# Where two key buffers begin: 128 bytes of room in front of each, in an attention and FFN kernel

## The chip, the core and the metric

The kernel runs on one core of a Trainium2 chip. Its time is the device time of one execution in microseconds; the time given for a kernel is the median of several executions. Beside the times there is a trace of one execution, taken by the hardware profiler, and all rows shown come from it. TensorE (PE) multiplies, with weight loads (PEld) issued by the same sequencer; VectorE (DVE), ScalarE (ACT) and GpSimd (POOL) do the rest; SyncE (SP) issues the DMAs.

## The reference

Attention over pooled keys and values, and behind it a two-layer FFN with softplus, all in float32:

```python
# q, k, v: (8 batches, 8 heads, 576 rows, 64); w_in: (512, 2048); w_out: (2048, 512)
k_p = k.reshape(B, H, 72, 8, D).mean(axis=3)      # 576 rows pooled to 72
v_p = v.reshape(B, H, 72, 8, D).mean(axis=3)
scores = (1 / sqrt(D)) * q @ k_p.transpose(0, 1, 3, 2)
scores = scores - scores.max(axis=-1, keepdims=True)
attn = exp(scores); attn = attn / (attn.sum(axis=-1, keepdims=True) + 1e-9)
x = heads side by side of (attn @ v_p)            # (8 * 576, 512)
h = x @ w_in
g = maximum(h, 0) + log1p(exp(-abs(h)))
out = g @ w_out                                   # (4608, 512)
```

## The kernel before

The 4608 rows of x are worked off in 18 chunks of 256 rows (`CT`), each in two tiles of 128. The chunks 0 to 2 go one way through the FFN (lines 619 to 646), chunk 3 mostly like the later ones but with line 713 for its second layer, and from chunk 4 on the FFN is the steady one: in eight steps, each with 24 matmuls of the first layer (`pair1`, line 672) and 21 of the second (`pair2_fast`, line 821), all with a weight of 128 x 128 and 256 columns streamed. Every product is made of three matmuls, of high and low parts.

While TensorE does the FFN of chunk c, it also does the attention of chunk c + 1 in between: the transposes of q (line 384), the scores (`pair_scores`, line 512), the transposes of the probabilities (lines 465 and 565) and the attention-value products (`av_products`, lines 591 and 598). In the chunks 0 to 3 the scores are line 404. A chunk has one stage of scores, of 64 matmuls; each takes 64 rows of the array, 64 columns, and streams 72 columns of keys:

```python
b = (x.first + i * P // 2) // S                                    # line 511: the batch of these 64 rows
o = nc.tensor.matmul(out=ps[r, n * SP:(n + 1) * SP], lhsT=x.q[js, m, r],
                     rhs=kT[b % 2][js, m], ...)
```

So the rows of an even batch read the buffer kT0, those of an odd batch kT1. As a batch has 576 rows, 2.25 chunks, some chunks lie in one batch and some in two. In a stage, all of the first tile's matmuls but one come ahead of the second tile's (`order` in `pair_scores`; the one head's two matmuls of the second tile stand at the two ends). The keys of a batch are pooled by DVE, transposed by TensorE (line 256) and written to kT by ACT (`k_scaled`, line 262), once for each batch.

The order of all work on TensorE, ACT, DVE and SP is written out by a planner (`Order`), which knows of each operation its engine, an assumed cost, what it follows and which slots it needs; it doesn't know where in memory a tile lies.

Where a tile lies follows from the order in which it is asked for. A pool puts its tiles one after the other, and the pools stand one behind the other: `const`, `wpool`, `xpool`, `one`, `small`. Tiles that no instruction reads or writes keep their bytes; the kernel uses such tiles (`fill`, line 220) to shift what comes after. In the program as built, these tiles begin at these bytes of each partition:

| tile | bytes | begins at | modulo 256 |
|---|---|---|---|
| kT0 (keys, even batches) | 1152 | 2240 | 192 |
| kT1 (keys, odd batches) | 1152 | 3392 | 64 |
| vs0, vs1 (values) | 1024 each | 4544, 5568 | 192 |
| vlo0, vlo1 (the last values) | 2048 each | 6592, 8640 | 192 |
| fill of 64 floats | 256 | 10688 | 192 |
| w (weights) | 90240 | 10944 | 192 |
| l (weights, staging) | 41088 | 102080 | 192 |

The other tiles come behind these. The q that the scores load as weights lies in two buffers at multiples of 512.

Of the kernel before, what the change touches and what calls it, by code (L numbers as in the profile page):

```python
# [9 lines left out]
F32 = mybir.dt.float32  # L10
# [98 lines left out]
def pooled_attention_softplus_ffn(  # L109
# [14 lines left out]
    P = 128  # L124
    POOL = 8
    SP = S // POOL
# [4 lines left out]
    HP = H // 2  # L131
# [10 lines left out]
    const = ctx.enter_context(tc.tile_pool(name="const", bufs=1))  # L142
    wpool = ctx.enter_context(tc.tile_pool(name="wpool", bufs=1))
# [42 lines left out]
    band(zl[:, 0:4 * KL].rearrange("p (n y) -> p n y", n=4), POOL, KM)  # L186

    SCALE = -1.0 / (POOL * D ** 0.5)
    kT = [const.tile([P, HP, SP], F32, name=f"kT{i}") for i in range(2)]

    vs = [const.tile([P, HP, D], F32, name=f"vs{i}") for i in range(2)]
    vlo = [const.tile([3 * 4 * KL, HP, P], F32R, name=f"vlo{i}") for i in range(2)]
# [4 lines left out]

    PART, ROOM, LATE = 2 * DM, 16, 5
    BEGINS = [0, FC - LATE, FC]
    FILL = 256 - ROOM, 32, 16, 64  # L200
    groups = [None, None]

    def group(f):
        g = 0 if f < FC - LATE else 1
        n = BEGINS[g + 1] - BEGINS[g]
        if groups[g] is None:
            groups[g] = wpool.tile([P, 2 * (n * PART + ROOM)], F32R, tag="wl"[g], name="wl"[g])
        return groups[g], f - BEGINS[g], n
# [9 lines left out]
        return w[:, (n + f) * PART:(n + f + 1) * PART]  # L218

    fill = lambda pool, n, i: n and pool.tile([P, n], F32, tag=f"fill{i}", name="fill")  # L220
    fill(wpool, FILL[3], 3)
    group(0)
    fill(wpool, FILL[0] - ROOM, 0)
    stage = wpool.tile([P, 2 * (LATE * PART + ROOM)], I32, tag="l", name="stage")
    stage_at = lambda i: stage[:, i * 2 * PART:(i + 1) * 2 * PART].rearrange("p (i n) -> p i n", i=2)
    fill(wpool, FILL[1], 1)
    for tag in ("Xha", "Xhb", "Xla", "Xlb"):
        xpool.tile([P, HP, CT], F32R, tag=tag, name="x")
    fill(xpool, FILL[2], 2)
    wi, wo = {}, {}  # L230
# [1332 lines left out]
```

## Time and profile before

| | us |
|---|---|
| median of 3 runs | 888.52 |
| lowest and highest run | 888.02, 890.73 |
| the profiled execution | 889.17 |
| its span, from the first to the last instruction | 887.4 |
| TensorE busy in the span | 874.7 |

In the rows of the profile, "PE h L672" is TensorE's work of line 672 on a tile named h, and x24 says how many instructions stand together. In the chain of waits each row has the start in us from the span's beginning, the length in us, and what ran; the length of a row is the time by which the chain moved on, so that a row of 24 matmuls divided by 24 is the distance from one matmul to the next. The duration of a single matmul in the groups is longer than this distance, as matmuls overlap.

### The profile page before, as it was taken

To read this page: it belongs to the slowest core of one execution; us is meant where nothing else is said; L and a number is where in the kernel's file an instruction comes from. 1 tells how busy PE (TensorE), PEld (TensorE's weight loads), DVE (VectorE), ACT (ScalarE), POOL (GpSimd) and SP (SyncE) were. 2 spreads that over 40 slices of the span, in tenths; PEclk is the share of its full clock that TensorE was granted. 3 is DMA by queue.
4 is the path that set the end of the run, shared out by engine and by line. 5 is a ranking of instruction groups with operands and counts; after the bars stand their busy time and mean duration, and the time that the engine had idled before them with its cause. 6 is when DMAs were issued, how large, how long until landed. Compare 5 with 4: busy or idle time off the path is not lost.

```text
span 887.4 us, 20500 instructions
## 1 busy us (share of the span) xinstructions
PE 874.7 (99%) x8280; PEld 831.5 (94%) x8280; DVE 645.2 (73%) x1601; ACT 417.9 (47%) x852; POOL 3.8 (0%) x33
## 2 busy tenths in 40 slices
PE   7999999999999999999999999999999999999997
PEld 3789989899899999999999999999999999999997
DVE  5899999888866868687767766778566564747454
ACT  5964433445454544544444445353545344444432
POOL 1000000000000000000000000000000000000000
PEclk9999999999999999999999999999999999999999
DMA  8975544545889678578757675677566556646472
GB/s 237 312 236 192 189 149 164 172 159 192 273 281 228 237 227 278 195 258 250 243 190 248 240 232 197 224 244 251 196 205 223 180 205 202 223 153 229 168 249 83
DMA packets 107086, 191.12 MB, mean 215 GB/s; under 512 B 46064, under 2 KB 60400, under 8 KB 106992
## 3 DMA queue, kind: packets, MB, share of 16 engines
q1 hardware_dynamic: 106992, 189.82, 63.6%
q8 instruction: 65, 1.06, 0.5%
q14 instruction: 29, 0.24, 0.1%
HBM read 167.25 MB, written 22.54 MB: 214 GB/s over the span
## 4 chain that ended last, share of the span: by engine, by line
PE 96%; DVE 1%; DMA 1%; ACT 1%; issue 0%; SPq 0%; DVEq 0%; ACTq 0%
PE h L672 38%; PE m L821 30%; PE acc L646 7%; PE h L624 7%; PE acc L713 3%; PE avp L591 2%; PE qTp L384 2%; PE ptp L465 2%; PE sc L512 1%; PE avp L598 1%; PE kps L1056 1%; DMA kvl<-in_v_dram 1%; DMA kvst<-in_k_dram 1%; ACT E L429 0%; PE m L512 0%; PE ltp L565 0%
## 5 line engine op out<-in xcount | busy, mean ns | idle before, releaser
L672 PE MATMUL h<-x,l 128*128 128x256 f32 x2748 | 337.9, 279 | 0.0
L672 PEld LDWEIGHTS h<-x,l 128*128 128x128 f32 x2748 | 323.9, 188 | 1.1
L680 ACT ACTIVATE g<-h 128x512 f32<-128x512 f32 x120 | 71.9, 599 | 267.4 <-PE h L672 267.2
L821 PE MATMUL m<-w,so 128*128 128x256 f32 x1134 | 148.3, 278 | 0.0
L821 PEld LDWEIGHTS m<-w,so 128*128 128x128 f32 x1134 | 138.3, 188 | 0.1
L731 DVE TENSOR_TENSOR sf<-g 128x128 f32<-128x128 f32 x112 | 32.7, 292 | 138.2 <-ACT g L680 138.2
L745 ACT CAST so<-sf 128x512 fp32r<-128x512 f32 x112 | 69.8, 623 | 69.2 <-DVE sf L734 68.4
L821 PE MATMUL m<-w,gh 128*128 128x256 f32 x476 | 91.9, 281 | 0.0
L750 DVE TENSOR_TENSOR so<-sf,so 128x512 fp32r<-128x512 f32 x112 | 77.3, 690 | 18.3 <-ACT so L745 16.6
L821 PEld LDWEIGHTS m<-w,gh 128*128 128x128 f32 x476 | 72.0, 188 | 0.0
L701 DVE TENSOR_TENSOR gl<-g,gh 128x384 fp32r<-128x384 f32 (+1 forms) x120 | 67.3, 561 | 2.6 <-ACT gh L694 2.6
L821 PE MATMUL m<-w,gl 128*128 128x256 f32 x238 | 66.1, 278 | 0.0
L694 ACT ACTIVATE gh<-h 128x384 fp32r<-128x384 f32 (+1 forms) x120 | 59.1, 493 | 0.0
L629 ACT ACTIVATE g<-h 128x256 fp32r<-128x256 f32 x96 | 32.0, 382 | 55.3 <-PE h L624 33.6
L624 PEld LDWEIGHTS h<-x,w 128*128 128x128 f32 x396 | 48.6, 188 | 2.7 <-ACT g L629 0.6
L624 PE MATMUL h<-x,w 128*128 128x256 f32 x396 | 49.8, 278 | 0.2 <-ACT g L629 0.2
L821 PEld LDWEIGHTS m<-w,gl 128*128 128x128 f32 x238 | 44.9, 189 | 0.0
L842 DVE TENSOR_TENSOR o<-o,m 128x256 f32<-128x256 f32 x98 | 39.8, 418 | 3.3 <-ACT o L834 0.4
L646 PE MATMUL acc<-w,g 128*128 128x512 f32 x132 | 41.9, 399 | 0.0
L821 PE MATMUL m<-l,gh 128*128 128x256 f32 x196 | 37.0, 278 | 0.0
L734 DVE TENSOR_TENSOR sf<-g,sf 128x128 f32<-128x128 f32 x112 | 32.7, 292 | 3.9
L435 DVE TENSOR_REDUCE sm<-E 128x8 f32<-128x576 f32 x30 | 21.2, 748 | 15.1 <-ACT E L347 15.1
(210 smaller groups left out, 1261.5 us busy)
## 6 DMA issues: line engine op xcount, KB each, us to landing
l<-wi SPq DMA_DIRECT2D x224, 512.0 KB
out_dram<-o SPq DMA_DIRECT2D x36, 256.0 KB
q<-in_q_dram SPq DMA_DIRECT2D x32, 256.0 KB
kst<-in_k_dram SPq DMA_DIRECT2D x24, 288.0 KB
vst<-in_v_dram SPq DMA_DIRECT2D x24, 256.0 KB
stage<-in_moe_w_in_dram SPq DMA_DIRECT2D x22, 256.0 KB
stage<-in_moe_w_out_dram SPq DMA_DIRECT2D x11, 512.0 KB
wi<-w SPq DMA_DIRECT2D x11, 512.0 KB
```

The costliest lines, as they stand in the source:

```text
L624: nc.tensor.matmul(out=ps[:, 0:CT], lhsT=row(w, kc), rhs=x[:, kc], start=first and kc == j == 0, stop=last and kc == KC - 1 and j == 2)
L646: nc.tensor.matmul(out=accs[c][t], lhsT=a[:, ts], rhs=w, start=f == 0 and j == 0, stop=f == FC - 1 and j == 2)
L672: nc.tensor.matmul(out=ps[:, k * CT:(k + 1) * CT], lhsT=row(w, kc), rhs=x_[c][i][:, kc], start=first and n == 0, stop=last and n == len(or ...
L680: nc.scalar.activation(out=g, in_=x.rearrange("p (b i) -> p b i", i=P), func=AF.Softplus)
L694: nc.scalar.activation(out=gh, in_=quarters(c, x.rearrange("p (b i) -> p b i", i=P)), func=AF.Softplus)
L701: nc.vector.tensor_tensor(out=gl, in0=quarters(c, g), in1=gh.bitcast(F32), op=ALU.subtract)
L731: tt(out=sf[:, 2], in0=g[:, 0], in1=g[:, 2], op=ALU.add)
L734: tt(out=sf[:, 3], in0=g[:, 3], in1=sf[:, 1], op=ALU.subtract)
L745: nc.scalar.copy(out=so[:, 0], in_=ss[c, u])
L750: nc.vector.tensor_tensor(out=so[:, 1], in0=sf, in1=so[:, 0].bitcast(F32), op=ALU.subtract)
L821: nc.tensor.matmul(out=ms[c][n], lhsT=x, rhs=y, start=u == 0 and j == 0 and n in (1, 6, 5, 4), stop=u == FP - 1 and j == 2 and n in (2, 7, ...
L842: nc.vector.tensor_tensor(out=o, in0=in0, in1=m[n], op=how)
```

## The change

Two tiles of 32 floats, which nothing uses, are asked for in the pool `const`, one in front of each buffer of keys. The fill of 64 floats in front of w is taken out.

```diff
-    kT = [const.tile([P, HP, SP], F32, name=f"kT{i}") for i in range(2)]
+
+    kT = []
+    for i in range(2):
+        const.tile([P, 32], F32, name=f"room{i}")
+        kT.append(const.tile([P, HP, SP], F32, name=f"kT{i}"))
...
-    FILL = 256 - ROOM, 32, 16, 64
+    FILL = 256 - ROOM, 32, 16
...
-    fill(wpool, FILL[3], 3)
     group(0)
     fill(wpool, FILL[0] - ROOM, 0)
```

## The prediction

> **What bounds the kernel now.** I read the page first: which engine is full, and what the chain that ended last is made of.
>
> ```profile
> span 887.4 us, 20500 instructions
> PE 874.7 (99%) x8280; PEld 831.5 (94%) x8280; DVE 645.2 (73%) x1601; ACT 417.9 (47%) x852; POOL 3.8 (0%) x33
> PE 96%; DVE 1%; DMA 1%; ACT 1%; issue 0%; SPq 0%; DVEq 0%; ACTq 0%
> ```
>
> TensorE is busy for 99% of the span, and 96% of the chain is its own work. No other engine has to get faster for a gain: each nanosecond by which two matmuls stand closer comes off the end. So the question is what the place of the keys does to TensorE. The keys are read in one kind of work, the scores, and the groups by tile tell how long these matmuls take (shortest, middle and longest, in ns).
>
> ```profile
> L512 PE MATMUL sc<-kT,qT x800: 222/223/273, 199.8 to 800.4; 64*64 64x72 f32 x160
> L512 PE MATMUL m<-kT,qT x96: 222/223/273, 285.1 to 800.4; 64*64 64x72 f32 x96
> ```
>
> The shortest and the middle one are 1 ns apart over all chunks, whichever buffer they read. 800 and 96 make 14 stages of 64 matmuls, one for each of the chunks 4 to 17. Nor is a whole stage longer with one buffer than with the other, as the chain of waits shows (start us, us, what), first for chunk 15, then for chunk 16:
>
> ```profile
> 705.75 0.21 PE m L512 x2
> ...
> 706.96 3.02 PE h L672 x24
> 709.98 2.47 PE m L821 x21
> 712.46 2.83 PE h L672 x24
> ...
> 734.76 2.83 PE h L672 x24
> ```
>
> ```profile
> 753.48 0.21 PE m L512 x2
> ...
> 754.69 2.93 PE h L672 x24
> 757.63 2.38 PE m L821 x21
> 760.01 2.72 PE h L672 x24
> ```
>
> From the first score matmul to the first FFN matmul both take 1.21 us. But what comes behind, the same instructions in the same order, differs. There are two paces: a matmul of line 672 takes 2.83 / 24 = 117.9 ns behind chunk 15's scores and 2.72 / 24 = 113.3 ns behind chunk 16's; on line 821 it is 2.47 / 21 = 117.6 and 2.38 / 21 = 113.3 ns. And the pace is held: chunk 15 is still at 2.83 some 28 us later.
>
> To see which chunks have which, I took 12 us of TensorE's time in each, from 1.8 us after the first score matmul on, where only lines 672 and 821 run (stretch, its length, busy us and matmuls, granted clock, DMA share, GB/s). The rows are chunks 6 to 17 in order:
>
> ```profile
> 286.90:298.90 12.00, 12.00 (x105) 1.00 0.83 305
> 334.63:346.63 12.00, 12.00 (x108) 1.00 0.84 281
> 380.91:392.91 12.00, 12.00 (x109) 1.00 0.74 265
> 426.85:438.85 12.00, 12.00 (x104) 1.00 0.64 234
> 474.00:486.00 12.00, 12.00 (x104) 1.00 0.85 290
> 521.03:533.03 12.00, 12.00 (x108) 1.00 0.65 219
> 568.03:580.03 12.00, 12.00 (x109) 1.00 0.75 263
> 613.97:625.97 12.00, 12.00 (x108) 1.00 0.66 231
> 661.55:673.55 12.00, 12.00 (x109) 1.00 0.60 224
> 707.48:719.48 12.00, 12.00 (x105) 1.00 0.59 220
> 755.21:767.21 12.00, 12.00 (x108) 1.00 0.61 220
> 801.16:813.16 12.00, 12.00 (x109) 1.00 0.60 220
> ```
>
> Chunks 6, 9, 10 and 15 fit in 104 or 105 matmuls, the others 108 or 109. The granted clock is 1.00 in all, and the DMA share sorts nothing: 0.59 stands in a long-paced row and 0.84 in a short-paced one. What does sort them is the buffer. A batch has 576 rows and a chunk 256, and a score matmul reads kT[b % 2], where b is the batch of its 64 rows (line 511). In chunks 6, 9, 10, 14 and 15 the whole first tile reads kT0. In 7, 8, 12, 13, 16 and 17 it reads kT1, and in 11 its second half does. So the long pace comes behind kT0 in four of five chunks and behind kT1 in none of seven. The exception, chunk 14, is also the one that comes to its scores at the long pace already:
>
> ```profile
> 654.51 2.83 PE h L672 x24
> ```
>
> I read it so: weight load and matmul can settle into either of two stable rhythms, the scores can throw them from one to the other, and from the short one kT0 throws them into the long one while kT1 leaves them where they are.
>
> **The change, part by part.** A room is 32 floats, 128 bytes of each partition; kT is 4 x 72 floats, 1152 bytes, which is 4.5 x 256, so that the buffers lie half of 256 apart now. kT0 goes from byte 2240 (192 modulo 256) to 2368 (64). kT1 goes from 3392 to 3648, both 64 modulo 256. vs and vlo move on by 256. The fill of 64 floats that is taken out, 256 bytes, takes that back: w begins at byte 10944 before and after, and all behind it stays.
>
> *Instructions, waits, queues:* none is added, removed or moved. Rooms and fills are read and written by nothing, no DMA touches the keys, and the planner's order depends on costs and not on bytes. 0 us. ACT writes kT to another place; at 47% it covers that.
>
> *The scores themselves:* 1.21 us a stage with either buffer. 0 us.
>
> *The pace behind kT0's scores:* kT0's new place is kT1's old one less 1024 bytes, so whatever repeats with 256, 512 or 1024 bytes meets there what gives the short pace now. The first group behind the scores then costs 2.93 for 3.02, each later one of line 672 saves 2.83 - 2.72 = 0.11, and each of line 821 saves 2.47 - 2.38 = 0.09. The other three long stretches, from their first group of line 672 to their last:
>
> ```profile
> 286.38 3.02 PE h L672 x24
> ...
> 314.18 2.83 PE h L672 x24
> ```
>
> ```profile
> 426.33 3.02 PE h L672 x24
> ...
> 448.04 2.83 PE h L672 x24
> ```
>
> ```profile
> 473.49 3.02 PE h L672 x24
> ...
> 501.29 2.83 PE h L672 x24
> ```
>
> Chunks 6, 10 and 15 each hold a first group, five more of line 672 and five of line 821: 0.09 + 5 x 0.11 + 5 x 0.09 = 1.09 us. Chunk 9's ends one pair earlier, at its transposes: 0.09 + 4 x 0.11 + 4 x 0.09 = 0.89. The sum is 3 x 1.09 + 0.89 = **4.16 us**. All of it lies on the chain, so nothing hides it; and with half a percent less time on TensorE, DVE at 73% doesn't come late.
>
> *vs and vlo, 256 bytes on:* the attention-value products read them, and behind those of chunk 6 the long pace goes on for three groups, this one and a group of line 821 on either side:
>
> ```profile
> 321.62 2.83 PE h L672 x24
> ```
>
> Their places stay the same modulo 256, and I take 0. The bounds are three groups, 2 x 0.09 + 0.11 = 0.29 us, gained in each of the four chunks whose products straddle two batches (6, 11, 13 and 15) or lost in each of the ten others: -1.2 to +2.9 us.
>
> The profiled execution took 889.17 us around its span of 887.4. Less 4.16 that is 885.01; the median of the runs, 888.52, lies 0.65 lower, and so does the prediction: **884.4 us**.
>
> The Trainium skill speaks against any effect. SBUF — State Buffer, Who interferes with whom, gives TensorE two read ports of its own and says "PE and ACT never wait on anyone"; TensorE: Matmul & The Clock Gate, Back-to-back issue gap, has N / 2.4 + 2.5 ns, an estimated 109 ns for 256 columns, with no term for an address. By these the sum would be 0. Two paces at one granted clock show that something is there which the formula lacks; that it is the address, no row shows directly.
>
> **The rivals.** *Chunk 14 turns.* It comes in at the long pace, and kT0's old place brought it back. If the new place keeps whatever pace it meets, as kT1's does with the short one, chunk 14 runs long like chunk 10 and costs 1.09: 885.5 us. Against it: chunk 13's second tile reads kT0 and moves too, so chunk 14 may be met at another pace.
>
> *No change.* The rhythm may hang on the instant at which the scores begin, as chunk 14 hints, and the long pace would only go to other chunks: 888.5 us. Against it: the rows of chunks 7, 8, 12, 16 and 17 agree with each other. It also comes if the change doesn't do what it says, the unread rooms taking no bytes; but the unread fill ahead of w does take its 256 in the program of before.
>
> *Slower: kT1's new place is a bad one.* If the pattern repeats with 512 bytes and not with 256, kT1 goes from 320 to 64 modulo 512, where neither buffer stood. Then chunks 7, 8, 11, 12, 13, 16 and 17 turn long, at up to 1.09 each: 7.6 us against 4.2 gained, 891.9 us. It decides from the fourth such chunk on (4 x 1.09 = 4.4). For it: nothing in the trace tells 256 from 512. Against it: the four slices of a buffer lie 288 bytes apart and stand at places all over 512 already, and yet each buffer acts as one.
>
> **How the numbers follow.** The forecast has 0.58, chunk 14 turning (with a loss or two of its kind) 0.16, no change 0.16, slower 0.10. A measurement of this kernel tells about 0.3%, 2.7 us, from no change, which puts the line at 885.9. The forecast and three quarters of the second case lie under it: 0.70 faster, 0.20 the same, 0.10 slower. The low end takes the forecast with the -1.2 of vs and vlo, and 0.6 for what one execution differs from the median: 882.6. The high end takes in no change and most of the +2.9: 888.9. Only kT1's bad place is left out.
>
> **What would show it.** In the same stretches of the changed kernel, moved by what was gained ahead of them: 108 or 109 matmuls in chunks 6, 9, 10 and 15; 2.72 and 2.38 in the chain behind their scores; stages of scores that still take 1.21 us. Chunk 14's row decides the first rival. If 104 or 105 stand where they stood, the place of kT0 is not the cause. If they stand in 7, 8, 12, 16 and 17, the place is the cause, but it doesn't repeat with 256 bytes. If the scores take longer, or DVE stands ahead of line 672 in the waits, the reading is wrong from its start.

## The result, and the profile after

The changed kernel takes 884.83 us in the median of 7 runs (883.18 to 886.72). The kernel before, run beside it again, takes 890.38 us in the median of 7 (888.02 to 891.61). The ratio is 0.9949, with a 95% interval of 0.9931 to 0.9967: half a percent faster, and clear of no change. The ratio is that of the means, which lie 4.5 us apart; the medians lie 5.55 us apart, because the single times fall into two groups (near 888.4 and 891 before, near 884.3 and 886.6 after) and the median of before comes from the upper one, that of the changed kernel from the lower one. The profiled execution is the one of 884.83 us. First its span, and then the score matmuls in the groups by tile:

```profile
span 883.1 us, 20500 instructions
```

```profile
L515 PE MATMUL sc<-kT,qT x800: 222/223/273, 200.8 to 796.0; 64*64 64x72 f32 x160
```

(The file is three lines longer ahead of them, so line 512 is now 515, 672 is 675 and 821 is 824.) The matmuls that read the keys last as long as before. The chain of waits behind chunk 15's scores, the stretch that stood at 2.83 and 2.47 before:

```profile
702.77 0.21 PE m L515 x2
...
703.99 2.93 PE h L675 x24
706.92 2.38 PE m L824 x21
709.30 2.72 PE h L675 x24
```

The stage itself is 703.99 - 702.77 = 1.22 us for 1.21. What comes behind it now runs at 2.72 and 2.38, 113.3 ns a matmul. And the twelve stretches of 12 us, 1.8 us after the first score matmul of the chunks 6 to 17 (stretch, length, busy us and matmuls, granted clock, DMA share, GB/s):

```profile
287.62:299.62 12.00, 12.00 (x108) 1.00 0.85 301
334.02:346.02 12.00, 12.00 (x109) 1.00 0.94 288
380.29:392.29 12.00, 12.00 (x108) 1.00 0.80 273
426.24:438.24 12.00, 12.00 (x109) 1.00 0.62 233
472.51:484.51 12.00, 12.00 (x108) 1.00 0.79 282
518.46:530.46 12.00, 12.00 (x109) 1.00 0.63 220
565.45:577.45 12.00, 12.00 (x108) 1.00 0.74 262
611.40:623.40 12.00, 12.00 (x109) 1.00 0.68 240
658.57:670.57 12.00, 12.00 (x109) 1.00 0.59 221
704.50:716.50 12.00, 12.00 (x108) 1.00 0.59 220
750.90:762.90 12.00, 12.00 (x109) 1.00 0.61 220
796.84:808.84 12.00, 12.00 (x108) 1.00 0.65 220
```

No chunk is left at 104 or 105. The short pace follows the scores in all twelve.

**Where the time went.** The span is 4.3 us shorter, 883.1 for 887.4. Up to the first score matmul of chunk 4 the changed kernel had lost 1.0 us (200.8 against 199.8 in the groups by tile); from there to the end it needs 883.1 - 200.8 = 682.3 us for 887.4 - 199.8 = 687.6, which is 5.3 us less. The four stretches of the prediction, 4.16, are in it. The rest is in three places that the sum had at nothing. The key transposes of chunk 13 no longer leave the long pace behind them, and the attention-value products of chunks 6 and 15 don't either; the first groups behind the scores of chunks 4 and 5 are the third place. Before, after chunk 13's key transposes:

```profile
626.85 2.52 PE m L821 x21
629.37 2.83 PE h L672 x24
632.20 2.47 PE m L821 x21
```

After, the same groups, and then the three behind chunk 6's products (2.55, 2.83 and 2.47 before):

```profile
624.27 2.45 PE m L824 x21
626.72 2.72 PE h L675 x24
629.44 2.38 PE m L824 x21
```

```profile
318.72 2.48 PE m L824 x21
321.20 2.72 PE h L675 x24
323.92 2.38 PE m L824 x21
```

With the group behind these rows (2.83 before, 2.72 after) the transposes give 0.38 us. The products give 0.07 + 0.11 + 0.09 = 0.27 in chunk 6 and as much in chunk 15. The first groups behind the scores of chunks 4 and 5 went from 3.02 to 2.94, and give some 0.2. Together: 4.16 + 0.38 + 0.54 + 0.2 = 5.3 us. Chunk 4's half of the 0.2 is not shown to come by the change: of the kernels below, the one with keys and values 256 bytes further has 2.94 there with the keys at the old places modulo 256, and the first of the map has 3.02 with them elsewhere.

### The profile page after: what moved, and what is told of

Its sections match the earlier page's. It is cut to its first block, busy times and chain, and to the rows that moved or that the text cites. A ratio compares the mean times of both kernels' runs of the same rounds, so it can differ in the third digit from the quotient of the medians.

```text
span 883.1 us, 20500 instructions
## 1 busy us (share of the span) xinstructions
PE 870.6 (99%) x8280; PEld 827.1 (94%) x8280; DVE 645.2 (73%) x1601; ACT 417.7 (47%) x852; POOL 3.8 (0%) x33
## 4 chain that ended last, share of the span: by engine, by line
PE 96%; DVE 1%; DMA 1%; ACT 1%; SPq 0%; issue 0%; DVEq 0%; ACTq 0%
PE h L675 37%; PE m L824 30%; PE acc L649 8%; PE h L627 7%; PE acc L716 3%; PE avp L594 2%; PE qTp L387 2%; PE ptp L468 2%; PE avp L601 2%; PE sc L515 1%; PE kps L1059 1%; DMA kvl<-in_v_dram 1%; DMA kvst<-in_k_dram 1%; ACT E L432 0%; PE m L515 0%; PE ltp L568 0%
```

## The experiments

In all of them the work, its order and its waits are those of the changed kernel, unless said otherwise, and only places in memory differ. Since the start of the execution scatters (below), I compare the time from chunk 4's first score matmul to the end as well: the span less the first start of the score matmuls in the groups by tile. It is called the rest of the span here, 687.6 us before and 682.3 us after. Each ratio is to the kernel before as it ran beside that experiment (medians of 888.51 to 888.94 us); where a kernel was run once, only its trace and the rest of its span are used.

### Both buffers at the old place of kT0

```diff
     kT = []
-    for i in range(2):
-        const.tile([P, 32], F32, name=f"room{i}")
-        kT.append(const.tile([P, HP, SP], F32, name=f"kT{i}"))
+    kT.append(const.tile([P, HP, SP], F32, name="kT0"))
+    const.tile([P, 32], F32, name="room1")
+    kT.append(const.tile([P, HP, SP], F32, name="kT1"))
+    const.tile([P, 32], F32, name="room2")
```

> Both buffers at 192 modulo 256, kT0's old place (kT0 at byte 2240, kT1 at 3520); values and all behind them as in the changed kernel. Theory (the place modulo 256 decides, 192 gives the long pace): the chunks of kT1 turn long too. In twelve us behind the scores 104 or 105 matmuls in chunks 7, 8, 11, 12, 13, 16 and 17 as well as in 6, 9, 10 and 15; some 6 us more than before (0.9 to 1.1 a chunk), near 1.007 of its time. Rival A (what counts is that both stand at the same place, wherever): as the changed kernel, 108 or 109 everywhere, 0.995. Rival B (the batch and not the place): as before, 6, 9, 10 and 15 long, 1.000.

Measured: 896.37 us in the median of 5, ratio 1.0083 (1.0068 to 1.0099); the rest of the span 895.1 - 201.0 = 694.1 us, 6.5 more than before. The stretches of chunks 8 and 14:

```profile
382.93:394.93 12.00, 12.00 (x104) 1.00 0.77 268
667.09:679.09 12.00, 12.00 (x109) 1.00 0.60 220
```

Chunk 8, of kT1, has turned long, and so has every chunk from 6 on but one. So it is the place and not the batch, and that both buffers stand at the same place is not what helps: at 192 they do so and the kernel is slower. The one that stays short is chunk 14, which comes to its scores at the long pace: as in the kernel before, it leaves them at the short one. (So it does in the changed kernel, at the good place.)

### The places exchanged

```diff
     kT = []
-    for i in range(2):
-        const.tile([P, 32], F32, name=f"room{i}")
-        kT.append(const.tile([P, HP, SP], F32, name=f"kT{i}"))
+    const.tile([P, 32], F32, name="room0")
+    kT.append(const.tile([P, HP, SP], F32, name="kT0"))
+    kT.append(const.tile([P, HP, SP], F32, name="kT1"))
+    const.tile([P, 32], F32, name="room2")
```

> The places modulo 256 exchanged: kT0 at 64 (byte 2368), kT1 at 192 (byte 3520); all behind them as in the changed kernel. Theory (192 gives the long pace): chunks 6, 9, 10 and 15 hold 108 or 109 matmuls in twelve us, and 7, 8, 12, 16 and 17, likely 11 and 13 too, hold 104 or 105; 7.0 us lost against 4.2 gained and 0.4 already lost before, about 1.002 to 1.003 of the time before. Rival A (same place for both decides): chunks 6, 9, 10 and 15 long as before, 1.000. Rival B (batch): the same four long.

Measured: 892.18 us in the median of 5, ratio 1.0035 (1.0021 to 1.0048); the rest of the span 890.9 - 201.9 = 689.0 us. Chunks 8, 9, 11 and 13:

```profile
382.44:394.44 12.00, 12.00 (x105) 1.00 0.78 272
429.47:441.47 12.00, 12.00 (x109) 1.00 0.63 234
521.69:533.69 12.00, 12.00 (x109) 1.00 0.68 217
616.10:628.10 12.00, 12.00 (x104) 1.00 0.68 241
```

The roles are exchanged with the places. Chunk 13, whose first tile reads kT1, turned long. Chunk 11, expected to, did not turn long behind its scores: there the first half of the first tile reads the good place and all that follows the bad one. But its key transposes, which read nothing that moved, then leave the long pace behind them, as chunk 13's did in the kernel before, where the first tile read the good place and the second the bad one:

```profile
534.30 0.26 PE kT L260 x4
534.56 2.52 PE m L825 x21
537.08 2.83 PE h L676 x24
```

So behind the scores themselves a bad place that only the later rows read is not seen here.

### Keys and values 256 bytes further

```diff
     kT = []
-    for i in range(2):
-        const.tile([P, 32], F32, name=f"room{i}")
-        kT.append(const.tile([P, HP, SP], F32, name=f"kT{i}"))
+    const.tile([P, 64], F32, name="room0")
+    kT.append(const.tile([P, HP, SP], F32, name="kT0"))
+    kT.append(const.tile([P, HP, SP], F32, name="kT1"))
```

> Keys and values 256 bytes further than before and nothing else: kT0 at 2496, kT1 at 3648, 192 and 64 modulo 256 as before, but 448 and 64 modulo 512 for 192 and 320. Theory (modulo 256): chunks 6, 9, 10 and 15 long, 104 or 105 matmuls, all others 108 or 109, time within 0.3% of before. Rival C (modulo 512 or more): another set of chunks. It also takes the move of the values out of the result: if the gain of the changed kernel came by that, this one has it too, 0.995.

Measured: 890.09 us in the median of 12, ratio 1.0006 (0.9993 to 1.0018); the rest of the span 890.6 - 203.0 = 687.6 us, as before. Chunks 8 and 9:

```profile
384.04:396.04 12.00, 12.00 (x108) 1.00 0.78 272
429.99:441.99 12.00, 12.00 (x105) 1.00 0.64 233
```

256 bytes change nothing, neither for the keys nor for the values that moved with them. So the gain is not from the move of the values, and for these places the pattern repeats with 256.

### The kernel before, with q 128 bytes further

```diff
+    q_room = {}
...
         def qT_out(self, ps, tag):
+            if "first" not in q_room:
+                q_room["first"] = one.tile([P, 32], F32, tag="qroom0", name="qroom0")
             self.q = one.tile([P, HP, P], F32, tag=tag, name="qT")
+            q_room.setdefault("tags", set()).add(tag)
+            if len(q_room["tags"]) == 2 and "last" not in q_room:
+                q_room["last"] = one.tile([P, 96], F32, tag="qroom1", name="qroom1")
```

> The kernel before with the keys where they were (192 and 64) and the two buffers of transposed q, which the scores load as weights, 128 bytes further (128 modulo 256 for 0); all behind them moves by 512. If the distance between streamed keys and loaded q decides, the roles swap: 104 or 105 matmuls in chunks 7, 8, 12, 16 and 17 (11 and 13 likely), 108 or 109 in 6, 9, 10, 14 and 15, 1.002 to 1.003. If the place of the keys alone decides, the pattern of before stays: 6, 9, 10 and 15 long, 1.000.

Measured: 890.12 us in the median of 10, ratio 1.0008 (0.9997 to 1.0020); the rest of the span 888.3 - 200.7 = 687.6 us. Chunks 8, 9 and 13:

```profile
381.16:393.16 12.00, 12.00 (x104) 1.00 0.80 260
428.19:440.19 12.00, 12.00 (x109) 1.00 0.66 239
614.43:626.43 12.00, 12.00 (x109) 1.00 0.69 243
```

The time is that of before, and by the time alone one would say that nothing happened. But the roles are exchanged, though no key has moved: chunk 9 is short now and chunk 8 long. So the place of the keys counts by where it lies to q. That the time is the old one is chance: five chunks at the long pace, 0.89 us for chunk 7 and 4 x 1.09 for 8, 12, 16 and 17, are 5.25 us more than the changed kernel, and the kernel before needs 5.3 more than it, by other chunks.

The expectation of 1.002 to 1.003 missed by the chunks 11 and 13, which were to turn long. Both lie in two batches, and both are short here from their scores to past their key transposes. With the places exchanged the distances from q to the keys were the same modulo 256, and chunk 13 was long from its scores on, chunk 11 from its key transposes on. So in these two chunks the distance modulo 256 is not the whole of it, and what else counts is open.

### Both keys at 64, and q 128 bytes further

The changed kernel with the edit to q of the last experiment.

> The changed kernel, both keys at 64, with the two buffers of transposed q 128 bytes further (128 for 0). If the distance from q to the keys modulo 256 decides, both are 192 from q now and nearly all chunks turn long as with both keys at 192: 104 or 105 matmuls in 6, 7, 8, 9, 10, 12, 15, 16 and 17 (11 and 13 open), 1.007 to 1.008 of the time before. If the place of the keys alone decides, all stay short, 0.995.

Measured: 897.0 us in the median of 4, ratio 1.0080 (1.0052 to 1.0107); the rest of the span 896.8 - 202.7 = 694.1 us, the very number of both keys at 192. Chunks 8 and 9:

```profile
384.59:396.59 12.00, 12.00 (x105) 1.00 0.80 266
431.61:443.61 12.00, 12.00 (x104) 1.00 0.64 228
```

The changed keys are good at 64 only because q begins at a multiple of 256. All chunks but 14 turned long, 11 and 13 too. So, but for the chunks 11, 13 and 14, it is the place of the streamed keys relative to the loaded q, modulo 256, that decides. I call it a distance; as q moved by just 128 bytes, half of 256, the sum of the two places would give the same four patterns as their difference, and no run here tells them apart.

### Six more places

Three kernels, each with kT0 and kT1 half of 256 apart as before, and the room behind kT1 such that the values stay as in the changed kernel. The diff is that of the first; in the second 24 and 40 floats stand for 16 and 48, in the third 40 and 24:

```diff
     kT = []
-    for i in range(2):
-        const.tile([P, 32], F32, name=f"room{i}")
-        kT.append(const.tile([P, HP, SP], F32, name=f"kT{i}"))
+    const.tile([P, 16], F32, name="room0")
+    kT.append(const.tile([P, HP, SP], F32, name="kT0"))
+    kT.append(const.tile([P, HP, SP], F32, name="kT1"))
+    const.tile([P, 48], F32, name="room2")
```

> A map of the places, the first of three: kT0 at 0 modulo 256, kT1 at 128, the values and all behind them as in the changed kernel. From 192 and 64, two ideas of the reason. Idea 1: a stream is bad whose first 64 bytes or so end at a 256-byte border; the four slices of a buffer begin at p, p + 32, p + 64 and p + 96, so the places 96 to 224 would be bad and 0 to 64 good: here chunks of kT1 (7, 8, 12, 16, 17) long, chunks of kT0 (6, 9, 10, 15) short. Idea 2: only places near 192 are bad: here all short, as in the changed kernel. If the distance to q modulo 256 were not what decides, any other pattern.

> The second: kT0 at 32 modulo 256, kT1 at 160. Idea 1 (96 to 224 bad): chunks of kT1 (7, 8, 12, 16, 17) long, those of kT0 (6, 9, 10, 15) short. Idea 2 (only near 192, by 32 at most): the same. Idea 2 in its narrow form (192 alone): all short.

> The third: kT0 at 96 modulo 256, kT1 at 224. Idea 1 (96 to 224 bad): both long, as with both at 192, 104 or 105 matmuls in twelve us in nearly all chunks, 6 to 7 us more than before. Idea 2 (near 192, by 32 at most): chunks of kT1 (7, 8, 12, 16, 17) long, those of kT0 short. Narrow form (192 alone): all short.

Measured, one time each: 885.0, 882.93 and 883.92 us; the rest of the span 682.5, 682.5 and 682.3 us. The stretches of chunk 8 (kT1) and chunk 10 (kT0), for the three kernels in turn:

```profile
380.44:392.44 12.00, 12.00 (x108) 1.00 0.76 263
472.66:484.66 12.00, 12.00 (x108) 1.00 0.88 294
```

```profile
378.37:390.37 12.00, 12.00 (x108) 1.00 0.79 263
470.59:482.59 12.00, 12.00 (x108) 1.00 0.85 291
```

```profile
379.37:391.37 12.00, 12.00 (x108) 1.00 0.74 264
471.59:483.59 12.00, 12.00 (x108) 1.00 0.87 294
```

All short: of the eight places at steps of 32 bytes, 192 alone is bad (with q at a multiple of 256). My first idea, that places 96 to 224 are bad because a stream's first 64 bytes end at a border of 256, has fallen, and so has its neighbour form. In these kernels the two buffers don't begin at the same place modulo 256, and they are as good as the changed one. The kernel before had one of its two buffers at the one bad place of eight.

### What is special about 192

In two kernels kT0's four slices are 512 bytes apart and not 288, so that all begin at one place modulo 256; kT1 is at 64 and the room behind it such that w stays where it was modulo 512. The diff is that of the first; the second has no room0 and a room1 of 32 floats.

```diff
     kT = []
-    for i in range(2):
-        const.tile([P, 32], F32, name=f"room{i}")
-        kT.append(const.tile([P, HP, SP], F32, name=f"kT{i}"))
+    const.tile([P, 16], F32, name="room0")
+    kT.append(const.tile([P, HP, P], F32, name="kT0")[:, :, 0:SP])
+    const.tile([P, 16], F32, name="room1")
+    kT.append(const.tile([P, HP, SP], F32, name="kT1"))
+    const.tile([P, 64], F32, name="room2")
```

> What is special about 192. The four slices of a buffer begin 288 bytes apart, so behind 192 they stand at 192, 224, 0 and 32 modulo 256. Here kT0's slices are 512 bytes apart and all begin at 0 modulo 256, where the slices of q begin; kT1 is as in the changed kernel, 64. If a slice at q's own place is what does it (at 192 it is the third), chunks 6, 9, 10 and 15 turn long, 104 or 105 matmuls in twelve us. If a slice at 192 does it, or the whole row of four places, they stay short, 108 or 109. Chunks of kT1 short in any case.

> The counterpart: kT0's slices 512 bytes apart and all at 192 modulo 256, kT1 at 64. If a slice that begins at 192 does it, chunks 6, 9, 10 and 15 turn long, 104 or 105. If a slice at q's own place does it, or the whole row 192, 224, 0, 32, they are short, 108 or 109.

Measured, one time each: 885.52 and 885.63 us; the rest of the span 683.4 and 682.4 us. Chunks 10 and 14 with all slices at 0, and then chunk 10 with all at 192:

```profile
472.19:484.19 12.00, 12.00 (x108) 1.00 0.85 283
658.25:670.25 12.00, 12.00 (x104) 1.00 0.63 221
```

```profile
473.29:485.29 12.00, 12.00 (x109) 1.00 0.82 287
```

Neither four slices at q's own place nor four at 192 throw a chunk that comes in short; the row of 192, 224, 0 and 32 does. So neither the first slice at 192 nor the third at 0 does it alone. Whether the second at 224 or the fourth at 32 would, no run here tells. One thing is new: with all slices at 0, chunk 14, which comes in long, stays long, and the rest of the span is 1.1 us more than in the changed kernel. This is the rival of the prediction, in a kernel where it happens.

### The values at other places

The changed kernel with the values 128 bytes further (64 modulo 256) and, in a second kernel, 32 bytes further (224); the room behind them moves w by 512 bytes.

```diff
+    const.tile([P, 32], F32, name="room2")        # 8 floats in the second kernel
     vs = [const.tile([P, HP, D], F32, name=f"vs{i}") for i in range(2)]
     vlo = [const.tile([3 * 4 * KL, HP, P], F32R, name=f"vlo{i}") for i in range(2)]
+    const.tile([P, 96], F32, name="room3")        # 120 floats in the second kernel
```

> The changed kernel with the values (vs and vlo, which the attention-value products load as weights) 128 bytes further, 64 modulo 256 for 192; w and all behind it 512 bytes further. What is left at the long pace in the changed kernel are the groups behind the products of chunks 11 and 13, which straddle two batches: 2.83 us for 24 matmuls. If the distance modulo 256 of loaded and streamed operands decides there too, the pace behind the products changes in some chunks: these two turn short (0.3 to 0.6 us gained), or others turn long (0.3 us each, up to 3 us). If only the scores have this, all stays: 2.83 in chunks 11 and 13, 2.72 in the others. The scores' chunks stay short in any case.

> The changed kernel with the values 32 bytes further (224 modulo 256 for 192), w and all behind it 512 bytes further. With the values at 64 other products left the long pace behind them than at 192; if, as with the keys, few places are bad, no products leave it here and chunks 11 and 13 go on at 2.72: some 0.8 us less TensorE time than the changed kernel, too little to be told from one time. If most places are bad for the values, two to four chunks have 2.83 behind their products.

Measured, one time each: 886.11 and 883.18 us; the rest of the span 682.9 and 682.1 us. With the values at 64, a group behind the products of chunk 6 and one behind those of chunk 13:

```profile
322.11 2.83 PE h L677 x24
...
328.29 2.83 PE h L677 x24
```

```profile
646.56 2.72 PE h L677 x24
```

So behind the attention-value products, too, the pace changes with places in memory: the long pace left chunk 13, stayed in chunk 11, and came to chunks 6 and 15, where it even lived through the transposes of q (328.29 in chunk 6; 2.83 in chunk 15 as well). Whether the distance to the streamed probabilities decides there, as it does for q and the keys, was not tried. With the values at 224, chunk 11's and 13's groups are still at 2.83, but the q transposes of chunk 13 end it:

```profile
643.85 2.83 PE h L677 x24
...
650.02 2.73 PE h L677 x24
```

None of the three places tried for the values, 192, 64 and 224, takes it from all chunks; what is left to gain, 0.29 us in chunk 11 and 0.52 in chunk 13 by the groups of the changed kernel, is under 1 us. A version that beats the changed kernel by more than these runs can tell was not found.

## Why the prediction was right

*The time.* 884.4 us was forecast and 884.83 measured; 4.16 us of gain were forecast, and 0.51% of 890.38 is 4.5 us. That they come this close is partly luck. The forecast started from 888.52, the median of three runs of before; from the 890.38 measured beside the changed kernel the same gain leads to 886.2. And the part that the change touches gained 5.3 us in the profiled executions, 1.1 more than the sum, of which 1.0 was lost again at the start, where runs scatter.

*The pace behind kT0's scores* went as its step said, group by group: 2.93 or 2.94 for 3.02, 2.72 for 2.83, 2.38 for 2.47 in chunks 6, 9, 10 and 15. The stages of scores still take 1.21 to 1.22 us. DVE came no later, at 73% before as after (the rest of the span would not have given back all of the 5.3 us).

*vs and vlo at nothing* was right for their own move (256 bytes further changed nothing, 687.6 us for 687.6) and wrong by what I left out: the pace at which a product stage is met counts as well as its places. The -1.2 us of the bound covered the 0.54 that came. With the values at 192 modulo 256, chunk 6's products left the long pace in every kernel in which they were met at it and the short one in every other. (Chunk 4's products straddle two batches as well, so the bound should have counted five such chunks and not four.)

*The key transposes of chunk 13* were not in the sum. They read nothing that moved (identity and pooled keys stayed where they were), and yet 0.38 us came there. The groups between the scores and these transposes run at 2.72 and 2.38 before as after, so no row shows a difference ahead of them. That the scores, whose second tile reads kT0, leave something behind that the distances don't show is my inference; chunk 11 with the places exchanged speaks for it, chunk 11 with q moved speaks against it (2.45 behind its key transposes, though its scores ended at the bad distance).

*"Whatever repeats with 256, 512 or 1024 bytes"* held for kT0; that 256 is enough, which kT1's new place hung on, is shown by the keys 256 bytes further. The rival in which kT1's new place is bad has fallen with it: chunks 7, 8, 12, 16 and 17 stand at 108 or 109.

*Chunk 14* did not turn. It came in long and went out short, at the new place as at the old one:

```profile
654.37 2.47 PE m L824 x21
...
658.05 2.92 PE h L675 x24
```

The reading behind that rival, that the good place keeps whatever it meets, was wrong for the steady chunks: it also turns long into short, and with the values at 64 it did so in chunks 7 and 16. Nor does it take kT0's old place to bring chunk 14 back: in every kernel in which chunk 14 came in long it went out short, except with all slices at 0. That it can go the other way, all slices at 0 have shown.

*"The place of kT0"* as the cause was right only in part. What decides, but for the chunks 11, 13 and 14, is the place of the keys relative to q, modulo 256, and one of the eight tried, 192, is bad; the prediction spoke of the keys' place alone, and no trace of before could have told the two apart, as q did not move. And that both buffers begin at the same place, a by-product of the change, is not what helps.

*The sum of 0* did not come. The formula that the prediction took from the Trainium skill, TensorE: Matmul & The Clock Gate, Back-to-back issue gap, is given there for an isolated matmul, and for a stream of weight loads and matmuls, as in this kernel, the section says that it miscounts at small and at large N. So it did not speak against two paces. The two independent read ports that the Trainium skill gives TensorE (SBUF — State Buffer, Who interferes with whom) did not keep the place of the keys from changing the rest of the span from 682.3 to 694.1 us, and the measurement decides; whether the ports have a part in it, no run shows.

*What stays open:* why a row of slices at 192, 224, 0 and 32 behind q, and none of the others, throws the weight loads and matmuls into the long rhythm; why chunks 11 and 13 went another way with the places exchanged than with q moved, at the same distances; whether it is the difference of the places or their sum; and what in TensorE keeps a rhythm over some 200 matmuls. The runs show when it comes, not what it is.

## What to carry to other kernels

Where TensorE is full, look not only at how long its matmuls take but at their distance, group by group, in the chain of waits: equal work at two paces under one granted clock may be time that can be had by moving a buffer, as it was here. Then find what sorts the paces (here, which of two buffers an earlier stage had read) and move that buffer by a part of the period (here 128 bytes of 256), with all else kept in its place; the trace tells more than the time does, as in the kernel with q moved, which had the old time and the opposite pattern. Here it was the place of the streamed operand relative to the loaded one that had to be kept, so a later move of either can bring the loss back (897.0 us).

## What the runs showed that I had not expected

An interruption of 1.2 us, itself of the same length either way, sets the pace of the 200 and more matmuls behind it, at 113.3 or 117.6 to 117.9 ns, and seven places of eight give the better one, with q at a multiple of 256.

Profiled executions of kernels with the same pattern differ mainly by their start. In the 14 profiled executions of this study the first score matmul of chunk 4 comes between 198.7 and 203.0 us, with no order by place. From there on, kernels with the same pattern agree to 0.2 us: 687.6 and 687.6 for the kernel before and the one 256 bytes further (the one with q moved has 687.6 with another pattern, by chance); 682.3, 682.5, 682.5, 682.3 and 682.4 for the changed one, the three of the map and the one with all slices at 192; 694.1 and 694.1 for the two with both keys at the bad distance. Differences far under the 0.3% that the whole time can tell can be read from this part alone. What scatters in the first 200 us was not looked into.
